# Attention and a SoLU feed-forward block in one float32 kernel: padded last key chunk, narrower weights-times-v products, one transpose for two ends, the product h times exp a round later, and the weight conversion spread over three engines

## The chip, the cores and the metric

The kernel runs on one core of a Trainium2 chip. The metric is the device time of one execution in microseconds; the median over several executions is compared. The engines are named as in the profile: PE (TensorE matmul), PEld (its weight loads), DVE (VectorE), ACT (ScalarE), POOL (GpSimd) and SP (SyncE, which here only issues DMAs).

## The reference

Eight batches of eight heads, 576 tokens, head size 64. Attention keeps only scores within `tau` of the row's largest; its output, as 4608 rows of 512, goes through a feed-forward block whose activation is h times softmax(h), followed by a layer norm. The weights `w_in` and `w_out` come in as float64 (64-bit words on the chip); all the rest is float32.

```python
scores = scale * np.matmul(q, k.transpose(0, 1, 3, 2))
thresh = np.max(scores, axis=-1, keepdims=True) - tau
scores = np.where(scores >= thresh, scores, -1000000000.0)
attn = np.exp(scores - max); attn = attn / (sum + 1e-09)
x = np.matmul(attn, v)          # (B,H,S,D) -> (B*S, H*D)
h = x @ w_in                    # (4608, 1024)
solu = h * (np.exp(h - h_max) / (sum + 1e-09))
ln = (solu - mu) / np.sqrt(var + 1e-06) * g_ln
out = ln @ w_out                # (4608, 512)
```

## The kernel before

**Rounds.** The order of the work is written out by hand: one loop, in which a pass is a round, records every engine's instructions in program order, and each engine runs its own in that order. There are 160 score rounds, 20 for each batch. A batch is cut into two halves of its queries. In half 0 each of four head pairs takes two rounds, in each of which one 128-query tile of either head is scored; in half 1 it takes three, the third for one tile that joins the last 64 queries of both heads (`q_ends`). The 576 keys are 4 chunks of 128 and a fifth of 64, the *end*.

**What a round records, in order.** `scores(r)` on PE (two tiles of 128 x 576); `maxes(r)` on DVE, and on POOL the threshold `nth` from them (L320); up to one extra job from a list (`x_next`: transposes of the next batch's q and k, `attend`, or transposes of u); the jobs in `early`; `exps(r)` on ACT (a Prelu pass that pushes scores under the threshold far down, L333, and an Exp pass that sums, L340); `normalise(r-1)` (POOL adds 1e-9, DVE inverts, POOL scales the weights, L349 to L352); the jobs in `late`; a quarter of a feed-forward tile on PE (`ff_h` L427 or `ff_o` L491, four matmuls); `blocks(r-1)`: DVE transposes the weights in 32 x 32 blocks into T (L366), and once a head pair (a *unit*) is complete, SP issues 16 DMAs that move the blocks into wT, keys on partitions (L374); a second extra job.

**Weights times v.** Five rounds after its last blocks, `attend` multiplies wT by v for both heads of the unit (L391): for each of 5 key chunks one matmul per head, 64 outputs wide, the two heads in the two halves of the array's columns. A unit of half 0 has 256 query columns. A unit of half 1 has 384 for each head: of the joint tile's 128 columns only 64 belong to the head, and the other 64 are computed and never read. The fifth chunk has 64 keys, so its matmuls use 64 rows of the array.

**Feed-forward.** A tile of 128 tokens takes four rounds: `ff_h` in two, then, one round after the second, `ff_max` (DVE L434, early), `ff_exp` (ACT L440, late) and straight behind it `ff_mul`, u = h times exp (DVE L446, late); `ff_stats` a round later.

**Buffers.** PSUM has three tiles of two banks (scores and h share them) and two single banks x0 and x1, shared by all transposes, weights times v and the output sums. A job that takes a single bank waits until the one before it in that bank has been read out. `qe` and `ke` hold the ends of q and k; each is transposed by a PE instruction of its own (L261), then read out by three DVE instructions (L265 twice, L269).

**Weight conversion.** Each of 16 pieces of 128 x 512 float64 values is turned into float32 in seven DVE passes: `weight_a` four (L194 to L204), `weight_b` three (L218 to L224). One piece is converted in each of the first 15 rounds, at the end of the round.

Of the kernel before, what the change touches and what calls it, by code (L numbers as in the profile page):

```python
# [8 lines left out]
F32 = mybir.dt.float32  # L9
# [11 lines left out]
def kernel(  # L21
# [50 lines left out]
    gs = const.tile([P, NC], F32, name="gs")  # L72

# [6 lines left out]
    q_ends = [const.tile([P, P], F32, name=f"q_end{x}") for x in range(NQE)]  # L80

# [20 lines left out]
    def load(b):  # L102
        d = {}
        for nm, src in (("q", q), ("k", k), ("v", v)):
            bufs = 2 if nm == "v" else 1
            e = loads.tile([ST, H, D], F32, tag=nm + "e", bufs=bufs, name=nm + "e")
            d[nm + "e"] = e
            if nm == "v":
                t = loads.tile([P, H, 4, D], F32, tag=nm, bufs=bufs, name=nm)
            else:  # L110
                t = loads.tile([P, 4, H, D], F32, tag=nm, bufs=bufs, name=nm)
            d[nm] = t
        batches[b] = d
        if b == 0:

            for h in range(H):
                for nm, src, queue in (("q", q, nc.sync), ("k", k, nc.scalar)):
                    queue.dma_start(
                        out=d[nm][:, :, h], in_=src[b, h, 0:SM, :].rearrange("(p t) d -> p t d", t=4)
                    )  # L120
                if h == 1:
                    for nm, src, queue in (("q", q, nc.sync), ("k", k, nc.scalar)):
                        queue.dma_start(
                            out=d[nm + "e"], in_=src[b, :, SM:S, :].rearrange("h p d -> p h d")
                        )
                    yield
        else:
            for nm, src in (("q", q), ("k", k)):
# [7 lines left out]
                nc.scalar.dma_start(  # L136
                    out=d[nm + "e"], in_=src[b, :, SM:S, :].rearrange("h p d -> p h d")
                )
                yield
# [4 lines left out]
        nc.scalar.dma_start(out=d["ve"], in_=v[b, :, SM:S, :].rearrange("h p d -> p h d"))  # L144
        yield

    def constants():
        make_identity(nc, ident)
        nc.gpsimd.memset(mhalf, -0.5)
        for t in q_ends:  # L150
            nc.gpsimd.memset(t, 0.0)
        nc.sync.dma_start(out=tau_t, in_=tau.partition_broadcast(P))
# [34 lines left out]
    def weight_a(x):  # L187
        if not wide:
# [9 lines left out]
        nc.vector.tensor_scalar(  # L198
            out=e, in0=e, scalar1=896.0, scalar2=0.0, op0=ALU.subtract, op1=ALU.max
        )  # L200
        nc.vector.tensor_scalar(
            out=e, in0=e, scalar1=255.0, scalar2=8388608.0, op0=ALU.min, op1=ALU.mult
        )
# [5 lines left out]
    def weight_b(x):  # L209
        d = raws.pop(x)  # L210
        _, dst, unit = piece(x)
        if not wide:
# [11 lines left out]
        nc.vector.scalar_tensor_tensor(  # L224
            out=dst, in0=dst, scalar=unit, in1=e.bitcast(F32), op0=ALU.mult, op1=ALU.mult
        )
# [13 lines left out]
    def prep(i, step):  # L240
# [19 lines left out]
        for x, nm in enumerate("qk"):  # L260
            nc.tensor.transpose(  # L261
                out=tp[:, ST * x : ST * x + ST], in_=src[nm + "e"][:, two], identity=ident[0:ST, 0:ST]
            )
# [47 lines left out]
    def maxes(s):  # L311
# [8 lines left out]
        nc.gpsimd.tensor_scalar(  # L320
# [35 lines left out]

    def blocks(s):
        b, half, hp, r = slots[s]
# [8 lines left out]
        if r == 1 + half:  # L367
            wT = work.tile([P, 5, 4, 32 * n], F32, tag="wT", name="wT")
            units[key]["wT"] = wT
            for step in range(4):  # L370
                for c in range(4):
# [3 lines left out]
                        out=wT[32 * c : 32 * c + 32, 0:nj, a, :],  # L375
# [3 lines left out]
    def attend(key):  # L379
# [5 lines left out]
        nq = 64 + 32 * half  # L385
        for c in range(5):
            kk = slice(0, P if c < 4 else ST)
            for h in range(2):
                vv = d["v"][:, 2 * hp + h, c] if c < 4 else d["ve"][:, 2 * hp + h]
                hh = slice(D * h, D * h + D)  # L390
                nc.tensor.matmul(  # L391
                    out=y[hh, 0 : 4 * nq], lhsT=vv, rhs=wT[kk, c, :, 64 * h : 64 * h + nq],
# [11 lines left out]
        yy = y[:, 0:384].rearrange("p (a t q) -> p a t q", a=4, t=3)  # L404
        h0, h1 = slice(0, D), slice(D, P)
        nc.scalar.copy(out=to[h0], in_=yy[h0, :, 0:2])  # L406
        nc.scalar.copy(out=to[h1], in_=yy[h1, :, 1:3])  # L407
        nc.vector.tensor_copy(out=e[h0], in_=yy[h0, 0:2, 2])  # L408
        nc.vector.tensor_copy(out=e[h1], in_=yy[h1, 2:4, 0])  # L409
# [129 lines left out]
    with tc.manual_schedule():  # L539
# [22 lines left out]
        early, late, next_late = [], [], []  # L562
        while True:
# [8 lines left out]
            elif not (ready or cur or prev or x_jobs or live or early or late or rnd <= max(pv_at)):  # L572
                break
# [9 lines left out]
            for job in early:  # L583
                job()
# [4 lines left out]
            for job in late:  # L589
                job()  # L590
            early, late, next_late = [], next_late, []
# [7 lines left out]
            elif quarter == 1:  # L599
                ff_h(cur, 1)  # L600
                quarter = 2
                early = [lambda t=cur: ff_max(t)]
                late.extend([lambda t=cur: ff_exp(t), lambda t=cur: ff_mul(t)])
                next_late = [lambda t=cur: ff_stats(t)]
# [5 lines left out]
            elif quarter == 3:  # L610
                if prev is not None:
                    ff_o(prev, 1)
                    late.append(lambda t=prev: ff_out(t))
# [51 lines left out]
```

## Time and profile before

| what | value |
|---|---|
| three runs | 1218.14, 1228.62, 1230.49 us (median 1228.62) |
| the profiled execution | 1225.07 us, span 1223.2 us |
| mean granted TensorE clock | 0.935 |
| PE, DVE, ACT, POOL busy | 1090.5, 690.2, 574.8, 350.8 us |

The span runs from the first to the last instruction; 1.9 us of the execution lie around it. In a view of groups a line gives source line, engine, operation, output and inputs, shapes and count, then busy time, mean duration and the idle time before with what ended it. For PE the shape begins with rows*columns of the array that are used. A float32 matmul leaves two records, so 8 records are 4 matmuls; a float32 transpose leaves one. In a timeline a line gives start, duration, engine and what ran, in brackets the idle time just before and what ended it. PEclk is the granted clock of TensorE as a share of full speed.

### The profile page before, as it was taken

To read this page: it belongs to the slowest core of one execution; us is meant where nothing else is said; L and a number is where in the kernel's file an instruction comes from. 1 tells how busy PE (TensorE), PEld (TensorE's weight loads), DVE (VectorE), ACT (ScalarE), POOL (GpSimd) and SP (SyncE) were. 2 spreads that over 40 slices of the span, in tenths; PEclk is the share of its full clock that TensorE was granted. 3 is DMA by queue.
4 is the path that set the end of the run, shared out by engine and by line. 5 is a ranking of instruction groups with operands and counts; after the bars stand their busy time and mean duration, and the time that the engine had idled before them with its cause. 6 is when DMAs were issued, how large, how long until landed. Compare 5 with 4: busy or idle time off the path is not lost.

```text
span 1223.2 us, 13714 instructions
## 1 busy us (share of the span) xinstructions
PE 1090.5 (89%) x4209; PEld 525.1 (43%) x4209; DVE 690.2 (56%) x1273; ACT 574.8 (47%) x1169; POOL 350.8 (29%) x801
## 2 busy tenths in 40 slices
PE   4675798889889899989998899989998899999988
PEld 2332343444434444444444444444444444444333
DVE  4887666645655556655655456654655456656322
ACT  2433255545554455544554455545554455554311
POOL 1222133323333233332333233332333223333200
PEclk9986889889997899989998899989997999999899
DMA  7377527632584247633485246633375233423400
GB/s 185 110 170 174 121 49 145 154 87 58 112 184 99 66 97 139 157 84 72 94 163 138 64 99 130 162 83 77 87 163 140 61 91 86 102 69 93 112 12 26
DMA packets 259304, 132.02 MB, mean 108 GB/s; under 512 B 96920, under 2 KB 252576, under 8 KB 259232
## 3 DMA queue, kind: packets, MB, share of 16 engines
q1 hardware_dynamic: 168752, 86.19, 32.2%
q10 hardware_dynamic: 90480, 44.97, 15.1%
q8 instruction: 34, 0.56, 0.2%
q14 instruction: 38, 0.31, 0.1%
HBM read 36.70 MB, written 9.44 MB: 38 GB/s over the span
## 4 chain that ended last, share of the span: by engine, by line
PE 53%; DVE 13%; DMA 9%; ACT 8%; SPq 6%; issue 5%; POOL 4%; ACTq 1%; DVEq 0%
PE o_ps L491 14%; PE h_ps L427 13%; PE pv L391 13%; PE s_ps L306 9%; SPq L374 6%; DMA wT<-T 5%; DVE T L366 5%; DVE nm L316 4%; ACT w L333 3%; POOL w L352 2%; ACT w L340 2%; DMA q<-in_q_dram 2%; PE tp_u L478 1%; ACT ob L498 1%; POOL nth L320 1%
## 5 line engine op out<-in xcount | busy, mean ns | idle before, releaser
L333 ACT ACTIVATE w<-s_ps,nth 128x576 f32<-128x576 f32 x288 | 199.3, 738 | 203.1 <-POOL nth L320 188.0
L491 PE MATMUL o_ps<-w,uT 128*128 128x512 f32 x576 | 274.7, 623 | 1.7 <-ACT uT L481 1.7
L316 DVE TENSOR_REDUCE nm<-s_ps 128x1 f32<-128x576 f32 x288 | 204.1, 743 | 104.7 <-PE s_ps L306 104.3
L366 DVE STREAM_TRANSPOSE T<-w 128x576 f32<-128x576 f32 x288 | 212.6, 767 | 86.5 <-POOL w L352 71.6
L306 PE MATMUL s_ps<-kT,qT 64*128 64x64 f32 (+1 forms) x1024 | 224.0, 483 | 35.9 <-ACT w L333 28.8
L352 POOL TENSOR_SCALAR w<-w,sm 128x576 f32<-128x576 f32 x288 | 211.4, 745 | 145.9 <-DVE sm L350 145.9
L427 PE MATMUL h_ps<-w,xh 128*128 128x512 f32 x512 | 243.5, 620 | 0.2 <-ACT w L333 0.2
L320 POOL TENSOR_SCALAR nth<-nm,tau_t 128x2 f32<-128x2 f32 (+1 forms) x160 | 47.7, 298 | 623.8 <-DVE nm L316 623.8
L340 ACT ACTIVATE w<-w,ntau 128x576 f32<-128x576 f32 x288 | 220.4, 772 | 1.0
L391 PE MATMUL pv<-wT,v 128*64 128x384 f32 (+1 forms) x1024 | 173.4, 488 | 36.2 <-issue 18.9
L306 PEld LDWEIGHTS s_ps<-kT,qT 64*128 64x128 f32 x1024 | 125.7, 203 | 172.5 <-issue 98.5
L491 PEld LDWEIGHTS o_ps<-w,uT 128*128 128x128 f32 x576 | 108.6, 198 | 130.4 <-issue 126.1
L427 PEld LDWEIGHTS h_ps<-w,xh 128*128 128x128 f32 x512 | 96.1, 198 | 112.2 <-issue 111.2
L391 PEld LDWEIGHTS pv<-wT,v 128*64 128x64 f32 x1024 | 78.7, 153 | 98.8 <-issue 70.3
L446 DVE TENSOR_TENSOR u<-h_ps,u 128x1024 f32<-128x1024 f32 x36 | 44.1, 1224 | 91.0 <-ACT u L440 91.0
L406 ACT COPY xh<-pv 64x256 f32<-64x256 f32 x32 | 11.7, 365 | 135.1 <-PE pv L391 135.1
L401 ACT COPY xh<-pv 128x256 f32<-128x256 f32 x32 | 11.9, 372 | 131.6 <-PE pv L391 128.6
L350 DVE RECIPROCAL sm<-sm 128x2 f32<-128x2 f32 (+1 forms) x160 | 26.1, 163 | 64.7 <-POOL sm L349 62.6
L408 DVE COPY xe<-pv 64x64 f32<-64x64 f32 x32 | 6.9, 215 | 97.9 <-ACT xh L407 97.9
L478 PE MATMUL tp_u<-ident,u 128*128 128x128 f32 x288 | 46.1, 284 | 15.9 <-DVE xe L409 7.1
L340 ACT ACTIVATION_READ_ACCUMULATOR w<-w,ntau 128x1 f32 x288 | 56.4, 196 | 0.0
L391 PE MATMUL pv<-wT,ve 64*64 64x256 f32 (+1 forms) x256 | 52.6, 491 | 0.0
(62 smaller groups left out, 726.2 us busy)
## 6 DMA issues: line engine op xcount, KB each, us to landing
wT<-T SPq DMA_DIRECT2D x512, 80.0 KB, 2.2
wT<-T SPq DMA_DIRECT2D x256, 100.0 KB, 2.3
wT<-T SPq DMA_DIRECT2D x256, 64.0 KB, 2.1
v<-in_v_dram ACTq DMA_DIRECT2D x8, 1024.0 KB, 6.6
out_dram<-ob ACTq DMA_DIRECT2D x32, 256.0 KB, 2.6
q<-in_q_dram ACTq DMA_DIRECT2D x28, 256.0 KB, 5.3
k<-in_k_dram ACTq DMA_DIRECT2D x28, 256.0 KB, 4.8
raw<-in_moe_w_in_dram ACTq DMA_DIRECT2D x8, 512.0 KB, 4.3
```

The source lines that it names most:

```text
L306: nc.tensor.matmul(out=ps[:, ks], lhsT=lhsT, rhs=kT[hh, ks], start=True, stop=True)
L316: nc.vector.tensor_reduce(out=nm[:, x : x + 1], in_=ps[:, 0:S], axis=AX.X, op=ALU.max, negate=True)
L320: nc.gpsimd.tensor_scalar(out=nth[:, 0:n], in0=nm[:, 0:n], scalar1=tau_t, scalar2=None, op0=ALU.add)
L333: nc.scalar.activation(out=w, in_=ps[:, 0:S], func=AF.Prelu, bias=d["nth"][:, x : x + 1], scale=1.0, alpha=1.0e30,)
L340: nc.scalar.activation(out=w, in_=w, func=AF.Exp, bias=ntau, scale=1.0, accum_out=sm[:, x : x + 1])
L352: nc.gpsimd.tensor_scalar(out=w, in0=w, scalar1=d["sm"][:, x : x + 1], scalar2=1.0, op0=ALU.mult, op1=ALU.mult,)
L366: nc.vector.transpose(out=T[:, :, place, :], in_=w)
L374: nc.sync.dma_start(out=wT[32 * c : 32 * c + 32, 0:nj, a, :], in_=T[32 * a : 32 * a + 32, c : NB : 4].rearrange("p j t q -> p j (t q)"),)
L391: nc.tensor.matmul(out=y[hh, 0 : 4 * nq], lhsT=vv, rhs=wT[kk, c, :, 64 * h : 64 * h + nq], start=c == 0, stop=c == 4,)
L427: nc.tensor.matmul(out=h[:, f], lhsT=x[:, c], rhs=w1[:, c, f], start=c == 0, stop=c == NP - 1)
L478: nc.tensor.transpose(out=tp[:, P * c : P * c + P], in_=d["u"][:, x : x + P], identity=ident)
L491: nc.tensor.matmul(out=d["o"], lhsT=d["uT"][:, c], rhs=w2[:, c], start=c == 0, stop=c == NC - 1)
```

## The change

1. v's end and the end chunk of wT become buffers of 128 partitions, allocated once, with partitions 64 to 127 zeroed at the start; so the fifth chunk's matmuls use 128 rows like the others. wT always has 160 columns in a block.
2. In half 1 a chunk's matmul of 384 columns per head becomes one of 192 and one of 128. The other 64 columns are not computed. One ACT copy reads both heads out, where there were two.
3. q's and k's ends share one tile of 128 partitions (`ends`), turned by one PE transpose.
4. `nth` is computed on DVE instead of POOL.
5. `ff_mul` moves from the late jobs of its round to the early jobs of the next.
6. Of the seven weight passes, two (the clamps of the exponent) go to ACT as Relu, and the last (scale and multiply) to POOL as two instructions.

```diff
+    wTs = [const.tile([P, 5, 4, 160], F32, name=f"wT{x}") for x in range(2)]
+    v_ends = [const.tile([P, H, D], F32, name=f"v_end{x}") for x in range(2)]
...
+        d["ends"] = ends = loads.tile([P, H, D], F32, tag="ends", bufs=1, name="ends")
...
+        sides = (("q", q, slice(0, ST)), ("k", k, slice(ST, P)))
...
+        for t in v_ends:
+            nc.gpsimd.memset(t[ST:P], 0.0)
+        for t in wTs:
+            nc.gpsimd.memset(t[ST:P, 4], 0.0)
...
-        nc.vector.tensor_scalar(
-            out=e, in0=e, scalar1=896.0, scalar2=0.0, op0=ALU.subtract, op1=ALU.max
-        )
-        nc.vector.tensor_scalar(
-            out=e, in0=e, scalar1=255.0, scalar2=8388608.0, op0=ALU.min, op1=ALU.mult
-        )
+        nc.scalar.activation(out=e, in_=e, func=AF.Relu, bias=lim[:, 0:1], scale=-1.0)
+        nc.scalar.activation(out=e, in_=e, func=AF.Relu, bias=lim[:, 1:2], scale=-8388608.0)
...
-        nc.vector.scalar_tensor_tensor(
-            out=dst, in0=dst, scalar=unit, in1=e.bitcast(F32), op0=ALU.mult, op1=ALU.mult
-        )
+        nc.gpsimd.tensor_scalar(out=dst, in0=dst, scalar1=unit, scalar2=1.0, op0=ALU.mult, op1=ALU.mult)
+        nc.gpsimd.tensor_tensor(out=dst, in0=dst, in1=e.bitcast(F32), op=ALU.mult)
...
-        for x, nm in enumerate("qk"):
-            nc.tensor.transpose(
-                out=tp[:, ST * x : ST * x + ST], in_=src[nm + "e"][:, two], identity=ident[0:ST, 0:ST]
-            )
+        nc.tensor.transpose(out=tp[:, 0:P], in_=src["ends"][:, two], identity=ident)
...
-        nc.gpsimd.tensor_scalar(
+        nc.vector.tensor_scalar(
             out=nth[:, 0:n], in0=nm[:, 0:n], scalar1=tau_t, scalar2=None, op0=ALU.add
         )
...
-        for c in range(5):
-            kk = slice(0, P if c < 4 else ST)
-            for h in range(2):
+        if half == 0:
+            parts = [(0, 0, 4, 0, 2, 0), (1, 0, 4, 2, 2, 0)]
+            wide_a = 64
+        else:
+            parts = [(0, 0, 2, 0, 3, 32), (1, 2, 4, 2, 3, 0), (0, 2, 4, 0, 2, 32), (1, 0, 2, 3, 2, 32)]
+            wide_a = 96
+        for c, x in [(c, x) for x in range(0, len(parts), 2) for c in range(5)]:
+            for h, a0, a1, first, n, shift in parts[x : x + 2]:
...
                 nc.tensor.matmul(
-                    out=y[hh, 0 : 4 * nq], lhsT=vv, rhs=wT[kk, c, :, 64 * h : 64 * h + nq],
+                    out=to[:, a0:a1, 0 : 32 * n], lhsT=vv,
+                    rhs=wT[:, c, a0:a1, 32 * first : 32 * first + 32 * n],
...
-        nc.scalar.copy(out=to[h0], in_=yy[h0, :, 0:2])
-        nc.scalar.copy(out=to[h1], in_=yy[h1, :, 1:3])
+        nc.scalar.copy(out=to, in_=yy[:, :, 0:2])
...
-                early = [lambda t=cur: ff_max(t)]
-                late.extend([lambda t=cur: ff_exp(t), lambda t=cur: ff_mul(t)])
-                next_late = [lambda t=cur: ff_stats(t)]
+                early.setdefault(rnd + 1, []).append(lambda t=cur: ff_max(t))
+                late.setdefault(rnd + 1, []).append(lambda t=cur: ff_exp(t))
+                early.setdefault(rnd + 2, []).append(lambda t=cur: ff_mul(t))
+                late.setdefault(rnd + 2, []).append(lambda t=cur: ff_stats(t))
```

Three places in the order of the instructions. **First, DVE in round 31 and the beginning of 32**, which returns once per batch: hm is the maximum of h, u the product h times exp, sm the inverse of the sums, T the block transposes, q_end and kT the read-out of the ends. Before:

```order
L316 TENSOR_REDUCE nm<-s_ps 128x1 x2
L434 TENSOR_REDUCE hm<-h_ps 128x1
L350 RECIPROCAL sm<-sm 128x1
L446 TENSOR_TENSOR u<-h_ps,u 128x1024
L366 STREAM_TRANSPOSE T<-w 128x18x32
L265 TENSOR_SCALAR q_end_84<-tp_e,scl 64x64 x2
L269 COPY kT<-tp_e 128x64
L316 TENSOR_REDUCE nm<-s_ps 128x1 x2
L350 RECIPROCAL sm<-sm 128x2
```

Now:

```order
L320 TENSOR_REDUCE nm<-s_ps 128x1 x2
L324 TENSOR_SCALAR nth<-nm,tau_t 128x2
L449 TENSOR_REDUCE hm<-h_ps 128x1
L354 RECIPROCAL sm<-sm 128x1
L373 STREAM_TRANSPOSE T<-w 128x18x32
L269 TENSOR_SCALAR q_end_85<-tp_e,scl 64x64 x2
L273 COPY kT<-tp_e 128x64
L320 TENSOR_REDUCE nm<-s_ps 128x1 x2
L324 TENSOR_SCALAR nth<-nm,tau_t 128x2
L461 TENSOR_TENSOR u<-h_ps,u 128x1024
L354 RECIPROCAL sm<-sm 128x2
```

The product has moved from ahead of the block transposes and the read-out of the ends to behind the next round's maxima, ahead of that round's reciprocal.

**Second, PE at a unit of half 1** (pv is weights times v). Before:

```order
L306 MATMUL s_ps<-kT,qT 128x512
L306 MATMUL s_ps<-kT,qT 128x64
L391 MATMUL pv<-wT,v 64x384 x8
L391 MATMUL pv<-wT,ve 64x384 x2
L250 MATMUL tp_q<-ident,q 128x128 x4
```

Now:

```order
L310 MATMUL s_ps<-kT,qT 128x512
L310 MATMUL s_ps<-kT,qT 128x64
L406 MATMUL pv<-wT_89,v 64x192 x8
L406 MATMUL pv<-wT_89,v_end_91 64x192 x2
L406 MATMUL pv<-wT_89,v 64x2x64 x8
L406 MATMUL pv<-wT_89,v_end_91 64x2x64 x2
L257 MATMUL tp_q<-ident,q 128x128 x4
```

Ten matmuls of 384 columns have become ten of 192 and ten of 128; the neighbours are the same.

**Third, DVE in round 2**, one of the rounds that convert a weight piece (em holds exponent and mantissa, raw the 64-bit words, w_74 the converted piece). Before:

```order
L316 TENSOR_REDUCE nm<-s_ps 128x1 x2
L350 RECIPROCAL sm<-sm 128x2
L366 STREAM_TRANSPOSE T<-w 128x18x32 x2
L218 SCALAR_TENSOR_TENSOR w_74<-raw,em 128x512
L221 SCALAR_TENSOR_TENSOR em<-raw,em 128x512
L224 SCALAR_TENSOR_TENSOR w_74<-w_74,em 128x512
L194 TENSOR_SCALAR em<-raw 128x512
L198 TENSOR_SCALAR em<-em 128x512
L201 TENSOR_SCALAR em<-em 128x512
L204 TENSOR_SCALAR em<-raw 128x512
```

Now, DVE and then ACT from the same round on:

```order
L320 TENSOR_REDUCE nm<-s_ps 128x1 x2
L324 TENSOR_SCALAR nth<-nm,tau_t 128x2
L354 RECIPROCAL sm<-sm 128x2
L373 STREAM_TRANSPOSE T<-w 128x18x32 x2
L226 SCALAR_TENSOR_TENSOR w_74<-raw,em 128x512
L229 SCALAR_TENSOR_TENSOR em<-raw,em 128x512
L205 TENSOR_SCALAR em<-raw 128x512
L212 TENSOR_SCALAR em<-raw 128x512
```

```order
L337 ACTIVATE w<-s_ps,nth 128x576 x2
L344 ACTIVATE w,sm<-w,ntau 128x576 x2
L195 DMA raw<-in_moe_w_in_dram 128x512
L210 ACTIVATE em<-em,lim 128x512
L211 ACTIVATE em<-em,lim 128x512
L263 ACTIVATE qT<-tp_q,scl 128x512
```

Three passes have left DVE and one small one (nth) has come to it; on ACT the two new passes stand between the issue of the next weight piece and the next round's read-out of q.

More of the change, by code (lines that the diff above doesn't have):

```diff
@@ L560 @@
         quarter = 0
-        early, late, next_late = [], [], []
+        early, late = {}, {}
         while True:
@@ L582 @@
             x_next(1 if rnd >= 4 else 2, rnd)
-            for job in early:
+            for job in early.pop(rnd, []):
                 job()
```

62 lines of the change are left out of this document (32 added, 30 removed).

## The prediction

> **What bounds the kernel now.** I read the page first, then busy time by stage, then the timeline around PE's longest gaps.
>
> ```profile
> PE 1090.5 (89%) x4209; PEld 525.1 (43%) x4209; DVE 690.2 (56%) x1273; ACT 574.8 (47%) x1169; POOL 350.8 (29%) x801
> ```
>
> PE by stage (start, length, busy, granted clock):
>
> ```profile
> 22.80:140.00 117.20, 77.40 (x247) 0.85 0.61 145
> 160.00:1150.00 990.00, 926.06 (x3702) 0.94 0.48 107
> ```
>
> No other engine comes near PE, but PE is not alone. Up to 140 us, where the weights are converted, it idles 39.8 us: another engine sets the pace there. Afterwards it idles 63.9 of 990 us and has a clock of 0.94. So time can be had from three places: PE's own columns, its gaps with the slow clock behind them, and the start. One gap, in time order:
>
> ```profile
> 538.42 1.30 PE L306 MATMUL s_ps<-kT,qT 64*128 64x512 f32 x8
> 538.93 1.10 ACT L440 ACTIVATE u<-h_ps,hm 128x1024 f32<-128x1024 f32 x1
> 540.16 1.22 DVE L446 TENSOR_TENSOR u<-h_ps,u 128x1024 f32<-128x1024 f32 x1 [3.22 <-ACT u L440]
> 541.30 0.77 DVE L366 STREAM_TRANSPOSE T<-w 128x576 f32<-128x576 f32 x1
> 541.99 0.54 DVE L265 TENSOR_SCALAR q_end<-tp_e,scl 64x64 f32<-64x64 f32 x2
> 542.54 0.23 DVE L269 COPY kT<-tp_e 128x64 f32<-128x64 f32 x1
> 542.87 0.69 PE L391 MATMUL pv<-wT,v 128*64 128x256 f32 x2 [3.16 <-issue]
> ```
>
> The profile calls the 3.16 us "issue", but pv starts 0.1 us after kT<-tp_e ends: it takes the PSUM bank that tp_e holds, and the read-out of tp_e stands on DVE behind the product u, which waits 3.22 us for ACT's exp. All long waits of this name are this place, once per batch:
>
> ```profile
> PE pv L391 <- issue: 18.9, 6, 3.2
> ```
>
> Behind each of the six the clock falls to half. The last of the six stretches, and their sum (PE alone):
>
> ```profile
> 961.20:964.60 3.40, 3.40 (x18) 0.51 0.67 149
> sum 51.00, PE 45.58; mean PE 7.60
> ```
>
> **The change part by part.** *The product a round later (5).* In round 31 and its like DVE no longer waits for exp. T can follow its input, which POOL has scaled long before; the two q_end and kT then need tp_e, which PE writes just before 538.42, and at 0.54 and 0.23 us they are done by about 539.4. PE's scores last until 539.72. The gap goes: **-18.9 us** (at least -12, should T wait a little). The product itself, 1.22 us, now stands ahead of the next round's reciprocal; behind that wait POOL's scaling, DVE's block transposes and SP's 16 DMAs. In that round PE has scores (1.30) and four matmuls of a feed-forward quarter (3.7) to do, and wT is needed only five rounds later, so I cost the delay at nothing; uncovered it would be 1.2 us for each of 36 tiles.
>
> *The clock.* 45.58 us of PE work done at half speed would take 22.8 at full speed. If the gap is what slows the clock, all of it comes back; if a new gap takes its place, nothing. The nearest row is another gap with the same consequence (gap, then the slow stretch):
>
> ```profile
> 367.02 3.02 PE L306 MATMUL s_ps<-kT,qT 64*128 64x512 f32 x8 [2.65 <-ACT w L333]
> ```
>
> ```profile
> 367.30:384.40 17.10, 15.23 (x44) 0.50 0.56 122
> ```
>
> so a gap of 2.65 us is enough, and none may be left near that size. I take four fifths: **-18 us** (0 to -22.8).
>
> *Columns and chunks (1, 2).* A unit of each half:
>
> ```profile
> 356.98 1.95 PE L391 MATMUL pv<-wT,v 128*64 128x256 f32 x16
> 358.86 0.65 PE L391 MATMUL pv<-wT,ve 64*64 64x256 f32 x4
> 359.44 3.70 PE L427 MATMUL h_ps<-w,xh 128*128 128x512 f32 x8
> ...
> 702.17 2.80 PE L391 MATMUL pv<-wT,v 128*64 128x384 f32 x16
> 704.90 0.86 PE L391 MATMUL pv<-wT,ve 64*64 64x384 f32 x4
> 705.69 3.70 PE L491 MATMUL o_ps<-w,uT 128*128 128x512 f32 x8
> ```
>
> From start to start four chunks take 1.88 us with 256 columns and 2.73 with 384: 0.2125 us for 128 columns, or 1.66 ns per column for both heads together (they run side by side). What is left is fixed: 1.88 - 4 x 256 x 0.00166 = 0.18 us where the array goes from 128*64 to 64*64, and 0.58 - 0.425 = 0.155 us where it goes on from there. With a fifth chunk of 128 rows one of these falls away: 0.17 us for each of 32 units of half 0. A unit of half 1 becomes 5 x (192 + 128) columns x 1.66 ns + 0.17 = 2.83 us instead of 3.52: 0.69 us, 32 times. Together 27.5 us at full clock; the first batch's units lie where PE is not the bound, so **-24 us**.
>
> This assumes that matmuls of 128 columns stream. They are not in the trace with 64 outputs; a transpose has 128 columns and a load of its own for each:
>
> ```profile
> 709.23 0.60 PE L250 MATMUL tp_q<-ident,q 128*128 128x128 f32 x4
> 709.67 1.19 PE L306 MATMUL s_ps<-kT,q_end 128*128 128x512 f32 x4
> ```
>
> ```profile
> L391 PEld LDWEIGHTS pv<-wT,v 128*64 128x64 f32 x1024 | 78.7, 153 | 98.8 <-issue 70.3 <-ACT ob L498 12.5 <-DMA wT<-T 4.0
> ```
>
> Four take 0.44 us, 0.110 each, as 128 x 1.66 x 0.5 = 0.106 would have it for one of a pair's two record slots. That speaks for streaming. The other bound: if the two heads' short records no longer ran side by side, a chunk's four would take 4 x 0.110 = 0.44 instead of 0.21 us, +36 us over 160 chunks, and the part would cost 9 us (-28 to +9).
>
> *The start (6, 4).* One round of DVE before:
>
> ```profile
> 68.69 1.42 DVE L316 TENSOR_REDUCE nm<-s_ps 128x1 f32<-128x576 f32 x2
> 70.82 0.17 DVE L350 RECIPROCAL sm<-sm 128x2 f32<-128x2 f32 x1 [0.71 <-POOL sm L349]
> ...
> 74.56 0.69 DVE L224 SCALAR_TENSOR_TENSOR w<-w,em 128x512 f32<-128x512 f32 x1
> 75.17 0.42 DVE L194 TENSOR_SCALAR em<-raw 128x512 int32<-128x512 int32 x1
> 75.63 0.43 DVE L198 TENSOR_SCALAR em<-em 128x512 int32<-128x512 int32 x1
> 76.09 0.43 DVE L201 TENSOR_SCALAR em<-em 128x512 int32<-128x512 int32 x1
> 76.43 0.42 DVE L204 TENSOR_SCALAR em<-raw 128x512 int32<-128x512 int32 x1
> 76.77 1.41 DVE L316 TENSOR_REDUCE nm<-s_ps 128x1 f32<-128x576 f32 x2
> ```
>
> DVE is never idle here but for POOL: the round lasts 8.08 us and is DVE's. L224 takes 0.61 of it (to 75.17), L198 and L201 0.80 (75.63 to 76.43): 1.41 us go. The 0.71 us before the reciprocal go too, since POOL's 1e-9 no longer queues behind nth; nth itself costs DVE about 0.16 (the reciprocal's row). In rounds with an end to read out that wait was already filled, so 9 of 14 gain 0.55 more: 14 x 1.41 + 9 x 0.55 = 24.7 us. POOL and ACT take the work over:
>
> ```profile
> 78.27 0.29 POOL L320 TENSOR_SCALAR nth<-nm,tau_t 128x2 f32<-128x2 f32 x1 [5.73 <-DVE nm L316]
> ```
>
> ```profile
> 78.59 0.74 ACT L333 ACTIVATE w<-s_ps,nth 128x576 f32<-128x576 f32 x1 [5.15 <-POOL nth L320]
> ```
>
> Both idle over 5 us of a round. POOL's two passes should cost 0.66 (a scaling of 128x576, L352, takes 0.745) and 0.66 to 1.32; ACT's two at most 0.74 each, as the 128x576 pass above. The Trainium skill (GPSIMD Engine Reference, 3.1 Elementwise) gives about 2.6 cycles per element for two inputs, an estimate of 1.1 us, which no run here shows; by it the start would come out the same.
>
> But ACT now waits for DVE's first pass at the end of a round, and behind it stand the read-out of q and k, the loads of the next batch and the Prelu pass. The loads matter:
>
> ```profile
> 105.00 0.47 PE L250 MATMUL tp_k<-ident,k 128*128 128x128 f32 x1 [6.02 <-DMA k<-in_k_dram]
> ```
>
> PE already waits for k here; its DMA is issued about 2 us later in the round, twice. With 1.3 us for the first Relu pair ahead of the first qT, some 6 us go: **-18 us** (-6 to -24).
>
> *Small parts.* One end transpose instead of two, one ACT copy fewer per unit of half 1, nth on DVE in later rounds: hidden behind PE's feed-forward matmuls (3.7 us) in most rounds; **-2 us** (-5, or +3 if DVE's 0.16 us per round is not covered).
>
> *Given back.* The bytes do not change, and PE already waits for wT at places:
>
> ```profile
> 371.91 3.68 PE L391 MATMUL pv<-wT,v 128*64 128x256 f32 x16 [1.87 <-DMA wT<-T]
> ```
>
> PE will be there sooner: **+5 us** (0 to +20, some 3 us a batch).
>
> Sum: -18.9 - 18 - 24 - 18 - 2 + 5 = -76 us, 1225 - 76 = 1149 for an execution like the profiled one. That lies 3.6 us under the median of the runs shown, between the second and the lowest; I say **1151 us**.
>
> **The rivals.** *A, short pairs pay for their loads.* If a record slot can't be shorter than its 64-column load, 0.153 us in the row above, the 128-column slot of 0.107 grows by 0.046, two per chunk: 160 x 0.092 = +15 us, 1166. Against it stand the transposes at 0.110 with wider loads. A page's rule goes the same way: the Trainium skill (TensorE: Matmul & The Clock Gate, Back-to-back issue gap) has 128-column matmuls in a stream of loads at about 81 ns rather than 56; by it, an estimate of +16 us. The transposes' row does not show it.
>
> *B, the gap moves.* The product delays reciprocal, scaling, transposes and DMAs of its new round; another bank or wT is late, the clock stays slow. Then the clock's 18 us and the gap's 19 are lost and the give-back is 20: 1151 + 18 + 19 + 15 = 1203. For it: DVE's round 32 has 1.42 + 0.16 + 1.22 + 0.17 us ahead of anything new. Against: no read-out of a bank follows the product there.
>
> *C, more clock comes back.* If the 2.65 us gaps shrink under what slows the clock (four such stretches; the one shown has 15.23 us of work at half speed), about 20 us more: 1130. The gap loses only POOL's hop, some 0.15 us.
>
> *D, slower than before.* Loads do not hide behind the short matmuls at all: in a half-1 unit 20 record slots each wait for a load of 0.153, 32 x 3.06 = +98 us, so 1151 + 98 = 1249. It decides from 0.12 us per slot (77 us lost over 640 slots). Against it: in the trace 64-column loads run under the other records of a chunk.
>
> **How the numbers follow.** Chances: forecast 0.62, A 0.12, B 0.12, C 0.11, D 0.03. The range 1115 to 1195 holds forecast, A, most of C and a part of B, and leaves out D and the rest of B. About 1% is what a measurement can tell from no change; of D nearly all is slower, B's tail gives the middle: faster 0.93, same 0.04, slower 0.03.
>
> **What would show it.** Right: a half-1 unit of 2.8 us and a half-0 unit of 2.3; no gap of 3.15 us before pv, full clock at the six places; the product no longer waiting 3.2 us on DVE; early rounds of 6.5 us. Wrong: half-1 units over 3.1 us (A or D); waits for wT or for DVE over 1 us at new places with half clock behind them (B); early rounds still near 8 us, paced by ACT or by k.

## The result and the profile after

| | before | changed |
|---|---|---|
| median, us | 1228.22 (1218.14 to 1230.49) | **1138.74** (1138.45 to 1140.66) |
| profiled span, us | 1223.2 | 1136.3 |
| PE busy / idle in the span, us | 1090.5 / 132.7 | 1030.7 / 105.6 |
| mean granted TensorE clock | 0.935 | 0.959 |

The ratio is 0.930 (95% interval 0.925 to 0.934): 7% faster. The forecast was 1151 us with a range of 1115 to 1195.

The first page of the changed kernel, busy time and granted clock in 40 slices:

```profile
PE 1030.7 (91%) x4817; PEld 555.1 (49%) x4817; DVE 712.0 (63%) x1385; ACT 581.9 (51%) x1169; POOL 345.7 (30%) x679
PEclk9986879889998999999998999999998999999989
```

PE is busy 59.8 us less, idle 27.1 us less; the two make up the 86.9 us of the span. The place of the long gap, in time order:

```profile
255.51 0.27 PE L267 MATMUL tp_e<-ident,ends 128*128 128x128 f32 x1
255.72 1.30 PE L310 MATMUL s_ps<-kT,qT 64*128 64x512 f32 x8
256.14 0.54 DVE L269 TENSOR_SCALAR q_end<-tp_e,scl 64x64 f32<-64x64 f32 x2
256.24 1.10 ACT L455 ACTIVATE u<-h_ps,hm 128x1024 f32<-128x1024 f32 x1
256.69 0.23 DVE L273 COPY kT<-tp_e 128x64 f32<-128x64 f32 x1
257.02 1.95 PE L406 MATMUL pv<-wT,v 128*64 128x256 f32 x16
258.64 1.22 DVE L461 TENSOR_TENSOR u<-h_ps,u 128x1024 f32<-128x1024 f32 x1
```

DVE reads tp_e out while ACT's exp still runs, the product starts 2.4 us after the exp did, and pv starts behind the scores with no wait. The windows there (PE) have a clock of 1.00; the first of the six:

```profile
255.50:262.30 6.80, 6.80 (x37) 1.00 0.48 104
```

A unit of half 1, from its first matmul to the next scores:

```profile
202.37 1.52 PE L406 MATMUL pv<-wT,v 128*64 128x192 f32 x16
203.72 0.49 PE L406 MATMUL pv<-wT,v_end 128*64 128x192 f32 x4
204.05 1.04 PE L406 MATMUL pv<-wT,v 128*64 128x128 f32 x16
204.92 0.39 PE L406 MATMUL pv<-wT,v_end 128*64 128x128 f32 x4
205.24 2.48 PE L310 MATMUL s_ps<-kT,qT 64*128 64x512 f32 x8
```

205.24 - 202.37 = 2.87 us, where 3.52 stood before and 2.83 was forecast. A unit of half 0 takes 257.02 to 259.32, 2.30 us (2.46 before, 2.29 forecast).

What pv waits for now (us in total, times, longest):

```profile
PE pv L406 <- DMA wT<-T: 9.4, 7, 2.8
PE pv L406 <- DMA ends<-in_k_dram: 6.6, 2, 3.7
PE pv L406 <- ACT ob L513: 1.1, 4, 0.4
```

The 18.9 us called "issue" are gone. The second line is read as wT too, for at both its places DVE's T, whose wait is for "wT<-T", starts within 0.15 us of pv. The first:

```profile
217.24 1.44 DVE L373 STREAM_TRANSPOSE T<-w 128x576 f32<-128x576 f32 x2 [6.67 <-DMA wT<-T]
217.28 3.68 PE L406 MATMUL pv<-wT,v 128*64 128x256 f32 x16 [3.71 <-DMA ends<-in_k_dram]
```

So the waits for wT went from 6.6 to 16.0 us. At the two places of the second line and at 849.15 us such a wait of 2.8 to 3.7 us had half clock behind it.

The start shows what was not foreseen. One round of DVE, and POOL's passes under it:

```profile
74.57 0.84 DVE L205 TENSOR_SCALAR em<-raw 128x512 int32<-128x512 int32 x1
75.33 1.48 DVE L212 TENSOR_SCALAR em<-raw 128x512 int32<-128x512 int32 x1
76.73 1.41 DVE L320 TENSOR_REDUCE nm<-s_ps 128x1 f32<-128x576 f32 x2
```

```profile
74.14 0.99 POOL L232 TENSOR_SCALAR w<-w 128x512 f32<-128x512 f32 x1 [1.47 <-DVE w L226]
75.22 1.31 POOL L233 TENSOR_TENSOR w<-w,em 128x512 f32<-128x512 f32 x1
```

L205 and L212 are the old L194 and L204, 0.42 us each before. Beside POOL's passes they take 0.84 and 1.48 us. While w_in was converted, rounds lasted 7.37 us (69.36 to 76.73) and, every other one, in which DVE also reads an end out, 8.23 us (61.14 to 69.36); with w_out they lasted 6.31 us (76.73 to 83.04). Before, w_in's all lasted 8.07 to 8.13 us.

### The profile page after: what moved, and what is told of

Same layout as the page of the kernel before. It is cut to its first block, busy times and chain, and to the rows that moved or that the text cites. A ratio compares the mean times of both kernels' runs of the same rounds, so it can differ in the third digit from the quotient of the medians.

```text
span 1136.3 us, 15132 instructions
## 1 busy us (share of the span) xinstructions
PE 1030.7 (91%) x4817; PEld 555.1 (49%) x4817; DVE 712.0 (63%) x1385; ACT 581.9 (51%) x1169; POOL 345.7 (30%) x679
## 4 chain that ended last, share of the span: by engine, by line
PE 65%; DVE 13%; DMA 10%; ACT 5%; SPq 3%; issue 2%; POOL 1%; ACTq 0%; DVEq 0%
PE h_ps L442 18%; PE o_ps L506 17%; PE pv L406 13%; PE s_ps L310 12%; DVE nm L320 3%; DMA wT<-T 3%; DVE T L373 3%; SPq L381 3%; ACT w L337 2%; PE tp_u L493 2%; DMA k<-in_k_dram 2%; DMA v<-in_v_dram 2%; DVE u L461 1%; ACT w L344 1%; POOL w L356 1%
## 5 line engine op out<-in xcount | busy, mean ns | idle before, releaser
L506 PE MATMUL o_ps<-w,uT 128*128 128x512 f32 x576 | 262.2, 599 | 2.0 <-ACT uT L496 2.0
L310 PE MATMUL s_ps<-kT,qT 64*128 64x512 f32 (+1 forms) x1024 | 215.1, 474 | 31.7 <-ACT w L337 26.6
L406 PE MATMUL pv<-wT,v 128*64 128x192 f32 (+2 forms) x1536 | 161.3, 351 | 17.4 <-DMA wT<-T 9.4
L406 PEld LDWEIGHTS pv<-wT,v 128*64 128x64 f32 x1536 | 110.1, 144 | 45.9 <-issue 21.6
L353 POOL TENSOR_SCALAR sm<-sm 128x2 f32<-128x2 f32 (+1 forms) x160 | 36.6, 229 | 125.6 <-ACT w L344 120.2
L421 ACT COPY xh<-pv 128x256 f32<-128x256 f32 x32 | 11.9, 372 | 122.8 <-PE pv L406 122.8
L417 ACT COPY xh<-pv 128x256 f32<-128x256 f32 x32 | 11.9, 372 | 92.6 <-PE pv L406 82.0
L406 PE MATMUL pv<-wT,v_end 128*64 128x256 f32 (+2 forms) x384 | 53.2, 338 | 0.0
L496 ACT COPY uT<-tp_u 128x512 f32<-128x512 f32 x36 | 21.1, 585 | 61.9 <-PE tp_u L493 56.2
L455 ACT ACTIVATE u<-h_ps,hm 128x1024 f32<-128x1024 f32 x36 | 39.8, 1105 | 24.8 <-DVE hm L449 24.8
L449 DVE TENSOR_REDUCE hm<-h_ps 128x1 f32<-128x1024 f32 x36 | 43.9, 1219 | 11.9 <-PE h_ps L442 11.7
```

The source lines that it names most:

```text
L310: nc.tensor.matmul(out=ps[:, ks], lhsT=lhsT, rhs=kT[hh, ks], start=True, stop=True)
L406: nc.tensor.matmul(out=to[:, a0:a1, 0 : 32 * n], lhsT=vv, rhs=wT[:, c, a0:a1, 32 * first : 32 * first + 32 * n], start=c == 0, stop=c == 4,)
L449: nc.vector.tensor_reduce(out=d["nm"], in_=d["h"], axis=AX.X, op=ALU.max, negate=True)
L455: nc.scalar.activation(out=d["u"], in_=d["h"], func=AF.Exp, bias=d["nm"], scale=1.0, accum_out=d["se"])
L506: nc.tensor.matmul(out=d["o"], lhsT=d["uT"][:, c], rhs=w2[:, c], start=c == 0, stop=c == NC - 1)
```

## The experiments

Times are compared with 1138.7 us. The kernel before took 1224 to 1226 us on the chips of these runs, and a kernel's own runs lie up to 10 us apart: differences under some 5 us are not read as differences of time. Busy and idle times of PE come from each run's profile.

**The product back in its old place**, all else changed:

```diff
-                early.setdefault(rnd + 2, []).append(lambda t=cur: ff_mul(t))
+                late.setdefault(rnd + 1, []).append(lambda t=cur: ff_mul(t))
```

> The changed kernel with the product h times exp back in its old place, late in the round after the feed-forward half; all else as changed. Theory (the product alone made the six gaps before pv, and these gaps alone made the slow clock behind them): six waits of pv of about 3.1 us come back, about 10 us of half clock behind each, +19 us of idle and +20 us of clock: 1175 to 1185 us, granted clock about 0.94. Rival (the clock came back because pv's matmuls are shorter, or because the start changed): the gaps cost their 19 us and no more, 1155 to 1161 us, granted clock still 0.955 or higher. Second rival (pv's shorter units now reach the place at another time, and the wait is taken elsewhere): under 1150 us.

Measured: 1178.7 us, ratio 0.963 (0.961 to 0.965).

```profile
PE 1041.2 (88%) x4817; PEld 561.4 (48%) x4817; DVE 706.0 (60%) x1385; ACT 582.5 (49%) x1169; POOL 345.3 (29%) x679
```

```profile
256.93 1.23 DVE L461 TENSOR_TENSOR u<-h_ps,u 128x1024 f32<-128x1024 f32 x1 [2.91 <-ACT u L455]
...
258.76 0.54 DVE L269 TENSOR_SCALAR q_end<-tp_e,scl 64x64 f32<-64x64 f32 x2
259.31 0.23 DVE L273 COPY kT<-tp_e 128x64 f32<-128x64 f32 x1
259.64 1.12 PE L406 MATMUL pv<-wT,v 128*64 128x256 f32 x4 [3.16 <-issue]
```

The six gaps are back, so the product's place alone makes them. In the span it costs 30.2 us of idle time (1177.0 - 1041.2 = 135.8, against 105.6) and 10.5 us of busy time with the same work, which is the clock. The time is as the theory said, the split between idle time and clock is not: more idle, less clock. Behind the six gaps the clock was half for 6.8, 3.4, 3.4, 0, 3.4 and 3.4 us, where the kernel before had 51 us in all.

**The product alone moved**, in the kernel before:

```diff
-                early = [lambda t=cur: ff_max(t)]
-                late.extend([lambda t=cur: ff_exp(t), lambda t=cur: ff_mul(t)])
+                early.append(lambda t=cur: ff_max(t))
+                late.append(lambda t=cur: ff_exp(t))
+                next_early = [lambda t=cur: ff_mul(t)]
```

> The kernel before with the product alone moved a round later; weights, columns and chunk as before. Theory (the six gaps alone made the six slow stretches, 51 us with 45.6 us of work in them): 18.9 us of idle and up to 22.8 us of clock come back: 1181 to 1188 us on a chip where the kernel before takes 1224, granted clock 0.95. Rival (the clock also depends on how much else PE idles nearby; with the product put back into the changed kernel its gaps had shorter slow stretches, 20 us instead of 51): 18.9 us of idle and about 12 us of clock: 1191 to 1198 us.

Measured: 1167.4 us, ratio 0.953 (0.950 to 0.956), 58 us less than before on that chip, outside both ranges.

```profile
PE 1066.3 (91%) x4209; PEld 512.8 (44%) x4209; DVE 698.0 (60%) x1273; ACT 574.6 (49%) x1169; POOL 352.6 (30%) x801
```

The work of PE is that of before, so the fall of its busy time, 1090.5 to 1066.3, is clock: 24.2 us. (The mean granted clock of this execution, 0.931, is not the 0.95 expected: it was 0.62 from 22.8 to 140 us, 0.85 before, where PE is not the bound; from 160 to 1150 us it was 0.97, 0.94 before.) Idle time fell by 32.6 us (132.7 to 1166.4 - 1066.3 = 100.1), not by 18.9. A second wait went with the first:

```profile
PE pv L391 <- ACT ob L498: 10.7, 13, 1.4
```

That is the kernel before; here the same line has 2.5 us in 4 waits. Such a place before and with the product moved:

```profile
301.43 1.39 DVE L316 TENSOR_REDUCE nm<-s_ps 128x1 f32<-128x576 f32 x2
...
306.02 0.68 ACT L498 ACTIVATE ob<-o_ps,rs 128x512 f32<-128x512 f32 x1
306.76 0.54 PE L391 MATMUL pv<-wT,v 128*64 128x384 f32 x2 [0.79 <-ACT ob L498]
```

```profile
291.69 1.30 PE L306 MATMUL s_ps<-kT,qT 64*128 64x512 f32 x8
293.02 1.42 DVE L316 TENSOR_REDUCE nm<-s_ps 128x1 f32<-128x576 f32 x2 [0.27 <-PE s_ps L306]
```

With the product moved, DVE takes the maxima at the moment the scores end (292.99). Before, they came 1.5 us after the scores' end at 299.93; ACT's passes and ob came later for it, and pv waited for ob's bank. With the product back in its old place in the changed kernel the same happens: pv waits 7.5 us for ob in 12 places, instead of 1.1 in 4. The two waits make 27.1 of the 32.6 us; another 4.0 are waits for k in the start.

**The columns: 384 again in half 1**, the padded chunk kept:

```diff
-            parts = [(0, 0, 2, 0, 3, 32), (1, 2, 4, 2, 3, 0), (0, 2, 4, 0, 2, 32), (1, 0, 2, 3, 2, 32)]
+            parts = [(0, 0, 4, 0, 3, 32), (1, 0, 4, 2, 3, 0)]
```

> The changed kernel, but the units of half 1 multiply 384 columns for both heads again, the eighth of them junk as before; the fifth chunk stays padded to 128 rows. Theory (PE is the bound outside the start, so every column costs 1.66 ns): a half-1 unit goes from 2.87 to about 3.36 us, 32 times, less the units of the first batch: +12 to +16 us, 1151 to 1155 us. Rival (PE's saved columns turn into waits for weights' chunks that come by DMA, so that they are worth little): the waits for wT shrink by as much as the matmuls grow, under +6 us.

Measured: 1144.6 us, ratio 0.936 (0.933 to 0.938).

```profile
PE 1043.6 (91%) x4177; PEld 514.8 (45%) x4177; DVE 712.6 (62%) x1385; ACT 582.2 (51%) x1169; POOL 345.3 (30%) x679
```

PE is busy 12.9 us more, as the theory has it; but it idles 7.2 us less (98.4 for 105.6), pv's waits for wT being 10.2 us instead of 16.0. So of 13 us of columns about half is paid back at the DMA: between the theory and its rival. The 5.9 us of time lie at the edge of what these runs resolve.

**The chunk: 64 rows again** in all 64 units:

```diff
+                kk = slice(0, P if c < 4 else ST)
...
-                    rhs=wT[:, c, a0:a1, 32 * first : 32 * first + 32 * n],
+                    rhs=wT[kk, c, a0:a1, 32 * first : 32 * first + 32 * n],
```

> The changed kernel, but the fifth chunk has 64 rows again (half the array) in all 64 units; the split of the columns stays. Theory (the change between 128 and 64 rows costs 0.15 to 0.18 us each time): half-0 units go from 2.31 to about 2.46 us, half-1 units, which pass the change twice now, from 2.87 to about 3.2 us: 32 x 0.15 + 32 x 0.33 = +15 us, 1150 to 1155 us. Rival (the junk columns were all that mattered and the fixed cost hides behind loads): half-0 units within 0.05 us of 2.31 and under +5 us in all.

Measured: 1154.5 us, ratio 0.946 (0.942 to 0.950). Half-0 units take 2.46 us again, half-1 units 3.32; PE is busy 1051.7 us, 21.0 more, and idles 4.4 less. The theory holds: rows that carry zeros cost nothing, leaving the full array costs 0.16 us in a half-0 unit and 0.45 in a half-1 unit, which here leaves it twice.

**All seven weight passes on DVE again**: L210 and L211, L232 and L233 replaced by the lines that the change removed.

> The changed kernel with all seven passes of the weights' conversion back on DVE. Theory (the start gained only 4 us of the 18 forecast because DVE's passes are stretched while POOL runs its own, because the first scores come later, and because k's DMA then sets the pace): little changes, 1136 to 1144 us, and the DVE passes of the conversion are back at 0.42 us; the first maxima come about 2 us earlier. Rival (the passes moved away were worth the 1.41 us a round that was counted, and something else in the start took it back): 14 x 1.41 = +20 us, 1155 to 1160 us.

Measured: 1141.8 us, ratio 0.933 (0.930 to 0.936). The rival falls: the four instructions on ACT and POOL are worth nothing that can be measured. DVE's rounds are 7.53 to 7.60 us, 0.5 under those of before (POOL's nth and the reciprocal behind it no longer queue), or, with an end to read out, 8.4, which is 0.3 over. And the first transpose of u, a mark for the end of the start, is where the changed kernel has it. In the kernel before, the changed one and this one:

```profile
194.16 0.63 PE L478 MATMUL tp_u<-ident,u 128*128 128x128 f32 x4 [1.43 <-DVE xe L409]
```

```profile
188.84 0.63 PE L493 MATMUL tp_u<-ident,u 128*128 128x128 f32 x4 [1.05 <-ACT w L337]
```

```profile
188.38 0.63 PE L498 MATMUL tp_u<-ident,u 128*128 128x128 f32 x4 [1.05 <-ACT w L342]
```

**POOL's two passes back to DVE, ACT's kept:**

```diff
-        nc.gpsimd.tensor_scalar(out=dst, in0=dst, scalar1=unit, scalar2=1.0, op0=ALU.mult, op1=ALU.mult)
-        nc.gpsimd.tensor_tensor(out=dst, in0=dst, in1=e.bitcast(F32), op=ALU.mult)
+        nc.vector.scalar_tensor_tensor(
+            out=dst, in0=dst, scalar=unit, in1=e.bitcast(F32), op0=ALU.mult, op1=ALU.mult
+        )
```

> The changed kernel with the last pass of the weights back on DVE as one pass; the two clamps stay on ACT; POOL has no pass of the weights. Theory (DVE's passes were stretched by POOL's, not by ACT's): the two shift-and-mask passes fall from 0.65 and 1.16 us to 0.42, a round takes about 6.7 us, and the whole 1134 to 1141 us, since k's arrival ends the start. Rival (ACT's passes stretch DVE's): they stay over 0.6 us. Second rival (the stretching was what the start lost): 1131 us or less.

Measured: 1135.0 us, ratio 0.926 (0.923 to 0.929). Groups of DVE from 60 to 100 us, the changed kernel and this one:

```profile
L212 DVE TENSOR_SCALAR em<-raw 128x512 int32<-128x512 int32 x6 | 7.0, 1163 | 0.0
L205 DVE TENSOR_SCALAR em<-raw 128x512 int32<-128x512 int32 x5 | 2.9, 589 | 0.0
```

```profile
L212 DVE TENSOR_SCALAR em<-raw 128x512 int32<-128x512 int32 x6 | 2.5, 421 | 0.0
L205 DVE TENSOR_SCALAR em<-raw 128x512 int32<-128x512 int32 x6 | 2.5, 420 | 0.0
```

With ACT still at work and POOL not, both passes are at 0.42 us: POOL stretched them, not ACT. Rounds are 6.6 us, 7.5 with an end, and the first tp_u stands at 183.27, 5.6 us earlier. (With one and the same start it stood at 185.41 and 183.57 in the two combined runs below, so some 2 us of such a shift mean nothing.) What of this reaches the end is under what these runs resolve.

**k loaded earlier**: two steps of the second batch's loads in a round.

```diff
-                next(iter(loading), None)
+                for _ in range(2 if loaded == 1 else 1):
+                    next(iter(loading), None)
```

> The changed kernel with the loads of the second batch issued two steps a round instead of one, so that k is asked for about two rounds sooner; nothing else. Theory (what the start saved on DVE was lost in waits for k: 2.7 + 2.2 + 4.1 + 0.5 + 2.2 = 11.7 us before the transposes of k and its ends): these waits go and the start ends 6 to 11 us earlier, 1127 to 1133 us. Rival (DVE's rounds set the pace of the start anyway and the waits for k run beside them): the waits move to the scores, which wait for the exp, 1135 to 1140 us.

Measured: 1144.1 us, ratio 0.933 (0.931 to 0.936). The theory falls. In the changed kernel PE's longest wait for k:

```profile
102.74 0.47 PE L257 MATMUL tp_k<-ident,k 128*128 128x128 f32 x1 [4.11 <-DMA k<-in_k_dram]
```

With k earlier no wait for k is left, but others have grown:

```profile
82.91 2.39 PE L310 MATMUL s_ps<-kT,qT 64*128 64x512 f32 x4 [7.76 <-ACT w L337]
102.63 1.11 PE L257 MATMUL tp_k<-ident,k 128*128 128x128 f32 x4 [6.54 <-ACT qT L263]
```

Both are waits for ACT, which issues these DMAs between its passes, as the rival has it, though the time is above its range; that the issuing makes ACT late is argued from the trace, not shown. The first tp_u comes at 190.40.

**The later batches' loads spread**, one DMA a round:

```diff
-                    if t % 2:
+                    if t % 2 or b > 1:
                         yield
```

> The changed kernel with the loads of q and k of the third and later batches issued one DMA a round instead of two; the same bytes in the same packets. Theory (the waits given back, 16.5 us of pv behind wT and half clock behind some of them, come from DMA engines that are 0.92 to 0.96 busy in the rounds in which the next batch's k is loaded): the peak is lower, pv's waits for wT fall to under 8 us, and the whole takes 5 to 12 us less: 1126 to 1133 us. Rival (the wT DMAs are late because the product and pv now come sooner, whatever else is on the queues): the waits stay over 12 us and the time within 3 us of 1138.

Measured: 1132.4 us, ratio 0.924 (0.921 to 0.927). PE's windows while the third batch's k is loaded, changed kernel; the fourth column is the share of the DMA engines:

```profile
196.00:202.00 6.00, 6.00 (x21) 1.00 0.92 157
202.00:208.00 6.00, 6.00 (x55) 1.00 0.96 185
208.00:214.00 6.00, 5.27 (x16) 1.00 0.92 190
```

With the loads spread the first has 1.13 and the last two 0.50 and 0.68, and pv's wait behind them is 0.88 us instead of 3.71. At this place the theory holds, for the whole kernel it does not: all of pv's gaps sum to 15.5 us (17.4 in the changed kernel), not to under 8, since shorter waits of up to 2.5 us appear in other rounds. The time fell all the same, by some 6 us, though the intervals of the two ratios still overlap, and the profiled execution, the longest of its four, idles only 1.4 us less.

**The gaps between scores filled**: five matmuls whose result nobody reads.

```diff
+    def warm():
+        tag, y = take_bank("warm")
+        banks_free.insert(0, tag)
+        for c in range(5):
+            nc.tensor.matmul(out=y, lhsT=ident, rhs=w2[:, c], start=True, stop=True)
...
+            if PER_BATCH <= rnd < NS and not busy and (quarter, prev) == (3, None):
+                warm()
```

> The changed kernel with five matmuls of 128x512 added, whose result nobody reads, in the four rounds whose PE gap of 2.62 us lies between two rounds of scores (226.7, 353.2, 602.3 and 858.0 us); no work of the kernel is changed. Theory (the clock goes to half because PE idles, and comes back late; four gaps of 2.6 us have 24 us of half clock behind them): 2.3 us of each gap are filled, the gaps shrink to 0.3 us, nothing becomes later, and the clock alone saves 8 to 12 us: 1126 to 1131 us, loss by the clock between the mean and the last scores from 25.6 to about 15 us. Rival (the slow clock belongs to the work that starts there, not to the idle time before it): the stretches stay, 1136 to 1141 us.

Measured: 1135.2 us, ratio 0.926 (0.924 to 0.929). PE behind the first of the four gaps, changed kernel and filled:

```profile
228.50:235.30 6.80, 6.00 (x24) 0.50 0.39 90
```

```profile
226.12 4.56 PE L559 MATMUL warm<-w,ident 128*128 128x512 f32 x10
```

```profile
228.50:235.30 6.80, 5.73 (x34) 1.00 0.37 88
```

The slow stretches at the four places are gone (23.9 us in the changed kernel), so it is the idle time ahead that slows the clock, and the rival's mechanism falls. The time, 3.5 us less, is under what these runs resolve and outside the theory's range. I had sized the filler wrongly: a matmul takes 0.91 us and not 0.46, so five lasted 4.56 us in a gap of 2.62. That takes four times 1.9 us back of some 12; but a shorter filler, below, did not bring them in.

**Three together** (POOL's passes back, loads spread, gaps filled):

> The changed kernel with three of the edits together: the last pass of the weights back on DVE (the clamps stay on ACT), q and k of the third and later batches loaded one DMA a round, and the five idle matmuls in the four gaps. If what each does alone adds up: 3 + 6 + 10 us less than 1138: 1115 to 1124 us. Rival (they share the same waits, since a faster stretch meets the same late DMA): 1124 to 1132 us.

Measured: 1119.5 us, ratio 0.913 (0.911 to 0.916), below the changed kernel's interval: 1.8% faster than it.

```profile
PE 1025.1 (92%) x4857; PEld 549.5 (49%) x4857; DVE 709.9 (63%) x1401; ACT 581.7 (52%) x1169; POOL 310.2 (28%) x647
PEclk9986889999999999999999999999999999999999
```

The three at least add up: 19 us together, where alone they had 3.7, 6.3 and 3.5, two of them under what these runs resolve. From the seventh slice on the clock is 90% or more in every slice. With three idle matmuls instead of five:

> The three edits together again, with three idle matmuls instead of five in each of the four gaps: five took 4.56 us, since one takes 0.91 us and not 0.46, and were longer than the gap of 2.62 us that they were to fill by 1.9 us; three take 2.74. Theory (the clock needs the gap filled and no more): the clock stays at 0.977 and four times 1.8 us of PE work go, 1110 to 1115 us. Rival (the longer filler also let the late wT and product land, so that shorter ones only bring waits back): 1117 to 1121 us.

Measured: 1119.7 us, ratio 0.914 (0.912 to 0.916): no difference, and the theory falls. pv's gaps sum to 15.5 us instead of 13.2, and between 195 and 1070 us half clock stands at 209.6, 370.0 and 748.9 us, where the longer filler had one such stretch. These rows fit the rival; its claim that the longer filler let wT and the product land was not tested by itself.

**nth on POOL again**:

```diff
-        nc.vector.tensor_scalar(
+        nc.gpsimd.tensor_scalar(
```

> The changed kernel with the small addition of the threshold (nth) back on POOL. Theory (on DVE it is 0.23 us hidden behind PE in the later rounds, but in the start POOL now has passes of 1.0 and 1.3 us ahead of it): the early rounds get longer by up to 1 us, later rounds do not change, and the whole is 3 to 12 us slower: 1141 to 1150 us. Rival (where the instruction stands does not matter, since k's arrival and the product set the pace): 1135 to 1140 us.

Measured: 1137.2 us, ratio 0.930 (0.926 to 0.933). No effect; the rival holds.

## Why the prediction was right, and where it was not

| step | forecast, us | measured, us | from |
|---|---|---|---|
| the six gaps of the product | -18.9 | -32.6 or -30.2 idle | product alone, or undone |
| the clock behind them | -18 | -24.2 or -10.5 busy, same work | product alone, or undone |
| columns and chunk | -24 | -6 and -16 | each undone |
| start | -18 | about -5 | first tp_u, 194.16 to 188.84 |
| small parts | -2 | 0 (nth) | nth undone |
| given back at wT | +5 | +9.4 | waits, 6.6 to 16.0 |

The mechanism of the largest terms was right, and the sum came within some 12 us of the result, but part of that is luck. Measured on the kernel before, the product with its clock was sized 21 us too low (58 for 36.9) and the start 13 us too high, and the two nearly cancel. Measured by undoing it in the changed kernel, the product is worth 40 us, near its 36.9, and it is the split between idle time and clock that was wrong. No single figure belongs to a term here, since the parts do not add up.

*The product and the clock.* The mechanism was right in each step: tp_e's bank, the read-out behind the product, half clock behind the gap, next to no new wait for the product's bank (0.4 us). The step that was mis-sized took the gap's own length as what its removal is worth. The row of 10.7 us of pv's waits for ob was in the page of before and I did not ask what made ob late; DVE's lateness behind the product did, and 8.2 us of it went with the gap. The fifth deducted from the clock's 22.8 us was not seen on the kernel before (24.2); undone in the changed kernel the clock was worth 10.5.

*Not additive.* The product is worth 58 us on the kernel before and 40 on the changed one; the other parts 45 without it and 29 with it. The clock accounts for most of the difference (24.2 us of busy time in one, 10.5 in the other): behind gaps of the same 3.15 us the half clock lasted 51 us in one kernel and 20.4 in the other. The four gaps of 2.65 and 2.62 us are alike: 47.8 us of slow clock before, 23.9 after. So part of rival C's gain came, though not in its way, since those gaps did not shrink. The product is not what did it: with the product alone moved they have 44.4 us, with it put back into the changed kernel 23.9. Nor is nth, with which on POOL again they have 23.9. What sets the length of a slow stretch, beyond the gap itself, stays open; with these same gaps single profiles of the other runs have from 17.1 us (all passes on DVE) to 37.5 (POOL's passes on DVE), so some of it may be chance.

*Columns and give-back.* Units came within 0.04 us of the forecast. Rivals A and D fall: matmuls of 128 columns stream. The Trainium skill (TensorE: Matmul & The Clock Gate, Back-to-back issue gap) would have had 81 ns for each instead of 56; by that rule a half-1 unit would take an estimated 3.3 us (2.83 and a 32nd of the 16 us of rival A). This trace disagrees: 2.87. About half of what the split of the columns freed on PE came back as waits for wT; that is most of the give-back, 9.4 us instead of 5. At one place its cause is shown: DMA engines 0.92 to 0.96 busy while the next batch's k is loaded, and a wait of 3.71 us that fell to 0.88 with the loads spread. Elsewhere spreading the loads moved the waits more than it removed them, and their cause stays open.

*The start.* This term failed, -18 us forecast and about -5 measured, none of it the product's (194.49 for the first tp_u with the product alone). The step that priced POOL's two passes (0.66, and 0.66 to 1.32; they take 0.99 and 1.31) took their time as hidden, which held in most rounds; what they do to DVE was not in the sum. They stretch two of DVE's passes from 0.42 to 0.84 and 1.48 us, so that w_in rounds went from 8.1 to 7.37 and 8.23 in turn, instead of 6.5. The Trainium skill (SBUF — State Buffer, Who interferes with whom) has the rule: some DVE instructions, tensor_scalar in its doubled mode among them, share a port pair with POOL, and the later of the two waits until the earlier has ended. The rows above agree for w_in: L212 begins at 75.33 and ends at 76.81, 0.28 us after POOL's pass of 75.22 to 76.53. For w_out they are divided: L212 ends at 83.11, 0.27 us after POOL's pass of 81.52 to 82.84, but L205 keeps its 0.42 us (at 81.95) beside that same pass. The prediction left the rule out.

Even so the eight rounds between the third and the eleventh maxima took 57.5 us instead of 64.9. But the first scores came 2.1 us later (first maxima at 24.98 instead of 22.88), and two later rounds were longer. That from 95.64 us, in which PE waits for k, lasted 10.9 us instead of 8.5. That from 120.33 us lasted 10.2 instead of 7.5: DVE waits 2.75 us there for ACT's second clamp, and ACT had waited 4.25 us for POOL's L232. So moved passes were waited for, which the sum had at nothing. Undoing all of the passes cost nothing, undoing POOL's alone moved the start 5.6 us forward. Bringing k earlier did not help; which wait of ACT's chain sets the end of the start stays open. Of the small parts only nth was undone by itself; the single transpose of the ends and the single copy were not.

*Rival B.* One of its signs came: waits for wT of over 1 us with half clock behind them (217.28, 344.28 and 849.15 us). Its cause did not: with the product alone moved, pv's waits for wT are 5.2 us (6.6 before), and with the product back in its old place in the changed kernel they are 18.0 (16.0).

## What to carry to other kernels

A gap of PE is priced by undoing it, not by its length: the 18.9 us of gaps were worth 40 us in one kernel and 58 in the other, with what stands late behind them and the slow clock. Work moved off a busy engine is priced on both sides: besides what the other engine takes, what its passes do to the first engine's own. And undo each part of a change by itself, since a sum that comes out right can hold two errors.

## What the runs showed of the hardware

PE's clock fell to half at gaps of 2.6 to 3.2 us, but not always for the same time: 3.4 to 17.1 us, and not at all at one of the gaps of 3.16 us (659.67 us, with the product back). Matmuls whose result nobody reads, put into the four gaps of 2.62 us, kept the clock at 1.00 there, and in the run of the three edits together no slice of the profile after the sixth fell under 0.9. And issuing a DMA seems able to hold an engine up. ACT in the changed kernel, with its DMA issues (ACTq):

```profile
68.89 1.02 ACTq L133 DMA_DIRECT2D q<-in_q_dram  x2
...
76.27 3.57 ACTq L133 DMA_DIRECT2D q<-in_q_dram  x2
...
79.94 1.37 ACT L337 ACTIVATE w<-s_ps,nth 128x576 f32<-128x576 f32 x2 [2.96 <-DMA wT<-T]
```

Two issues of one source line took 1.02 us in one round and 3.57 in the next. The Prelu pass behind them starts 0.1 us after they end, although its threshold was ready on DVE at 78.41. This is read from one place; no run tests it.
